# Hash bits on 32 rows, one weight tile converted behind attention, and first products ordered by feature half

## The chip, the cores and the metric

The kernel runs on one core of a Trainium2 chip. The metric is the device time of one execution in microseconds; the median of three runs is 713.83 us (713.04 to 716.22). The engines are called PE (matrix products; PEld is its weight load), DVE (vector), ACT (scalar), POOL (GpSimd) and SP (which issues most DMAs).

## The reference

Three stages follow each other. The inputs are q, k, v of shape (2, 8, 768, 64); the weights of the first mixture stage are 64-bit floats.

```python
q_bits = (np.einsum('bhsd,dk->bhsk', q, proj) > 0).astype(np.int64)      # 6 bits
k_bits = (np.einsum('bhsd,dk->bhsk', k, proj) > 0).astype(np.int64)
mask = q_bucket[:, :, :, None] == k_bucket[:, :, None, :]                # equal bits
scores = np.where(mask, scale * np.matmul(q, k.transpose(0, 1, 3, 2)), -1000000000.0)
attn = softmax(scores); attn_out = np.matmul(attn, v)
x = attn_out as (1536 tokens, 512)
x = (x @ w_a) * (x @ w_b) @ w_out                                        # 512 x 1536, 1536 x 512
out = the better of 8 experts per token: gate * relu(x @ w1[e]) @ w2[e]
```

## The kernel before

**Attention** works on eight pairs of heads. A pair's queries and keys are turned so that 128 rows hold the 64 features of both heads. `units` are (pair, head, group): 48 units of 256 queries, six to a pair. For each unit the loop of `attention` issues, for two halves of 128 queries each: scores (`scores`, L270 and L273) into one of two PSUM tiles "s", a row maximum on DVE (`rowmax`, L278), an exponential on ACT (`expo`, L284), a normalisation on POOL (`normal`, L301) and a transposition on DVE (`turn`, L308). Two units in three (u % 3 is 0 or 2) also have half of a head's product with v on PE (`pv`, L320). The third (u % 3 is 1) has a preparation for a later pair in its place: either `turned` (12 transposes, L114) or `signs` (L233, L246). The outputs of a preparation are taken by ACT in the next unit, ahead of pv. PE, DVE, ACT, POOL and SP each run their instructions in the order in which this loop writes them.

**The mask** is added to the scores as a matrix product of signs. Multiplying q and k by the projection (`lz`, its 6 columns placed in a strip for each head, zeros elsewhere) gives rows of bits; a Sign activation makes them +1 and -1 (`qf`, `sk`), and `kf` is the key signs times a large factor, one copy for each head j with zeros on the other head's rows. In a score tile (768 keys as two halves n) the scores of half n are a product on 64 rows at tile position (64n, 0), and the mask's product follows on the same 64 rows: row group n needs the query signs for all queries, so the signs of the two query halves stand in `QF` on one row group and, copied by two DMAs (L240), in `QG` on the other. For pair 0 `opening` writes them directly with ACT (L166).

**The first mixture stage** begins inside attention. `load_first` and `split64` convert weight tiles of 64-bit floats to a high and a low 32-bit part in steps that `plan` hangs on points (u, at) of the loop: fetch, rest, top (DVE), low (ACT), add (POOL), size (ACT), guard (DVE), parts (an ACT cast and a POOL subtraction). Four tiles are the first 256 columns of w_a and w_b in halves f = 0, 1 of 128 features; two more are the halves of w_out. Tiles are staged in `spare` (mid's buffers "g") or `late` (attention's buffer "raw"). `fill` says where products of the first 768 tokens (`gated_products`, L597) are issued inside and behind the loop, taken from the list `first` in order; their outputs can be `held` until a later point. Behind the loop (NU = 48) come the last pv pieces, the last epilogue, the remaining products, and then the mixture stages, where PE's order is a long list.

Of the kernel before, what the change touches and what calls it, by code (L numbers as in the profile page):

```python
# [25 lines left out]
class Kernel:  # L26
# [8 lines left out]
    def constants(self, const):  # L35
        nc = self.nc
# [8 lines left out]
        nc.vector.tensor_scalar(p[:, 1:2], p[:, 0:1], 5, 1, ALU.logical_shift_right, ALU.bitwise_and)  # L45
        nc.vector.tensor_scalar(p[:, 0:1], p[:, 0:1], 31, None, ALU.bitwise_and)
# [12 lines left out]
        self.lz = const.tile([128, 2, 2, 32], F32, name="lz")  # L59
# [4 lines left out]
    def attention(self, xh, xl, pools, hook):  # L64
# [9 lines left out]
        for tag, shape, dt, n in (  # L74
            ("et", [128, NC * S], F32, 2), ("e", [128, 2 * S], F32, 3), ("vr", [128, NC * 256], F32, 2), ("raw", [128, 2 * S], F32, 1),
            ("q", [128, S], F32, 2), ("qs", [128, S], F32, 2), ("k", [128, S], F32, 2), ("ks", [128, H2], F32, 2),
            ("xp", [128, S], F32, 2), ("co", [128, S], F32, 2), ("qf", [128, H2], BF16, 2), ("qg", [128, H2], BF16, 2), ("kf", [128, S], BF16, 2), ("sk", [128, H2], BF16, 1),
        ):
            sb.tile(shape, dt, tag=tag, name=tag, bufs=n)
        raw, Q, QS, K, KS, QF, QG, KF, VR = {}, {}, {}, {}, {}, {}, {}, {}, {}  # L80
# [56 lines left out]
        def opening():  # L137
# [6 lines left out]
            for t, tag in ((QF, "qf"), (QG, "qg")):  # L144
                t[0] = sb.tile([128, H2], BF16, tag=tag, name=tag, bufs=2)
# [39 lines left out]
            for x, r in enumerate(half):  # L185
                nc.tensor.matmul(
                    pvb[1][r, 0, :H2], lz[:, r], K[0][:, x * H2:(x + 1) * H2], start=True, stop=True, tile_position=(0, 64 * x)
                )
            sign(sk, pvb[1][:, 0, :H2])
            nc.tensor.matmul(pvb[0][:, 0, :H2], lz, Q[0][:, keys], start=True, stop=True)  # L190
            for x in range(2):
                sign((QF, QG)[x][0][half[x]], pvb[0][half[x], 0, :H2])
            for j in range(2):
                nc.vector.tensor_scalar(KF[0][:, j], sk, self.fac[:, j:j + 1], None, ALU.mult)
# [4 lines left out]
            def rest():  # L199
                nc.tensor.matmul(pvb[0][:, 1, :H2], lz, Q[0][:, queries], start=True, stop=True)  # L200

                def out(*_):
                    for x in range(2):
                        sign((QF, QG)[1 - x][0][half[x]], pvb[0][half[x], 1, :H2])
# [7 lines left out]
        def masks(eng=nc.scalar):  # L212
            for kf, sk in later:
                for j in range(2):
                    if eng is nc.scalar:
                        eng.mul(kf[:, j], sk, self.fac[:, j:j + 1])
                    else:
                        eng.tensor_scalar(kf[:, j], sk, self.fac[:, j:j + 1], None, ALU.mult)
            later.clear()

        def signs(i, n):
            p = pvb[n]
            lz = self.lz.rearrange("p a b c -> p (a b c)")
            half = [slice(64 * x, 64 * x + 64) for x in range(2)]

            def sign(dst, src):
                nc.scalar.activation(dst, src, AF.Sign, bias=self.bias[:src.shape[0]], scale=2.0 ** 100)

            if n == 0:
                QF[i] = sb.tile([128, H2], BF16, tag="qf", name="qf", bufs=2)  # L230
                QG[i] = sb.tile([128, H2], BF16, tag="qg", name="qg", bufs=2)
                for x, r in enumerate(half):
                    nc.tensor.matmul(  # L233
                        p[r, 0, :H2], lz[:, r], Q[i][:, x * H2:(x + 1) * H2], start=True, stop=True, tile_position=(0, 64 * x)
                    )

                def out(*_):
                    sign(QF[i], p[:, 0, :H2])
                    for x in range(2):
                        nc.sync.dma_start(out=QG[i][half[1 - x]], in_=QF[i][half[x]])  # L240

                return out
            KF[i] = sb.tile([128, 2, H2], BF16, tag="kf", name="kf", bufs=2)
            sk = sb.tile([128, H2], BF16, tag="sk", name="sk", bufs=1)
            for x, r in enumerate(half):
                nc.tensor.matmul(  # L246
                    p[r, 0, :H2], lz[:, r], K[i][:, x * H2:(x + 1) * H2], start=True, stop=True, tile_position=(0, 64 * x)
                )

            def out(*_):  # L250
                sign(sk, p[:, 0, :H2])
# [10 lines left out]
        def scores(u, t):  # L262
# [98 lines left out]
        for j in range(2):  # L361
            d = slice(64 * j, 64 * j + 64)
            for x in range(2):
# [13 lines left out]
        for u in range(NU + 2):  # L377
# [35 lines left out]
            if new < len(pairs):  # L413
                preps, held, held_kind = [kind(new, x) for x in ((1, 0) if kind is turned else (0, 1))], new, kind
# [46 lines left out]
class Experts:  # L461
# [16 lines left out]
    def split64(self, src, shape, dest, scratch=None):  # L478
# [45 lines left out]
        def parts():  # L524
# [3 lines left out]
            nc.gpsimd.tensor_tensor(l, v, f32(h), ALU.subtract)  # L528
# [32 lines left out]
    def load_first(self, which, f, scratch):  # L561
# [15 lines left out]
        return self.split64(src, shape, dest, scratch)  # L577
# [515 lines left out]
def tile_kernel(ctx, tc, q, k, v, proj, w_a, w_b, w_out, emb, tau, w1, w2, out, dbg=None):  # L1093
# [5 lines left out]
    with tc.manual_schedule():  # L1099
# [15 lines left out]
        with tc.tile_pool(name="conv", bufs=1, side="left") as X.conv, \  # L1115
# [10 lines left out]
            jobs = [X.load_first(w, f, spare) for f in range(2) for w in range(2)]  # L1126
            outs = [X.load_first(2, f, late) for f in range(2)]
# [224 lines left out]
```

## Time and profile before

| what | value |
|---|---|
| median of 3 runs | 713.83 us (713.04 to 716.22) |
| profiled execution | 712.7 us |
| its span, first to last instruction | 710.9 us |
| PE busy | 693.8 us (98%) |
| DVE busy | 453.6 us (64%) |
| ACT busy | 355.7 us (50%) |
| POOL busy | 435.4 us (61%) |
| mean granted PE clock | 0.998 of full speed |

The span runs from the first to the last instruction; 1.8 us of the profiled execution lie around it. Busy times of PE and PEld overlap. A row of the timeline gives a start, a duration, the engine, the line of the kernel and the operation, output and inputs, the shapes, how many instructions were merged, and in brackets how long the engine idled before it and what ended that. The profile models the end of a matmul: of one shown 0.48 us long the next may start 0.32 us behind it.

### The profile page before, as it was taken

The page shows a single profiled execution, that of the slowest core. Times are in us where ns is not written, and L with a number is a line of the kernel's source. Part 1 is how long each engine was busy: PE and PEld are TensorE (multiplying, and loading weights), DVE is VectorE, ACT ScalarE, POOL GpSimd, SP SyncE. Part 2 cuts the span into 40 slices and gives each one's busy share as a digit, 9 for nine tenths or more (in the row PEclk, how much of TensorE's full clock was granted, in tenths as well). Part 3 has the DMA queues.
Part 4 walks back from the last instruction along what each step waited for, and adds up shares of the span by engine and source line. Part 5 has one row for each costly group of instructions (what it writes and reads, how often), then busy time and mean ns, then how long its engine had stood idle before and what let it go on. Part 6 is the DMA issues. An engine that isn't in the chain of part 4 may idle for free.

```text
span 710.9 us, 16289 instructions
## 1 busy us (share of the span) xinstructions
PE 693.8 (98%) x6796; PEld 583.5 (82%) x6796; DVE 453.6 (64%) x623; ACT 355.7 (50%) x660; POOL 435.4 (61%) x439
## 2 busy tenths in 40 slices
PE   8899999999999999999999999999999999999996
PEld 5465656566689999999999999988889899989995
DVE  4899999999966636546546456335646756556640
ACT  4789888988744341211212121234546565555560
POOL 1789999989964735636726537454525766657651
PEclk9999999999999999999999999999999999999999
DMA  6947754743241311211303201633533865676500
GB/s 151 211 106 182 162 126 116 171 114 96 47 136 60 120 61 60 67 52 60 119 0 108 71 12 48 234 108 104 169 110 101 284 229 197 205 258 226 208 37 24
DMA packets 68444, 88.00 MB, mean 124 GB/s; under 512 B 28931, under 2 KB 41027, under 8 KB 68368
## 3 DMA queue, kind: packets, MB, share of 16 engines
q1 hardware_dynamic: 63728, 78.41, 37.4%
q0 software_dynamic: 2560, 7.34, 2.7%
q10 hardware_dynamic: 2080, 1.18, 0.6%
q8 instruction: 54, 0.88, 0.5%
q14 instruction: 22, 0.18, 0.1%
HBM read 75.52 MB, written 7.34 MB: 117 GB/s over the span
## 4 chain that ended last, share of the span: by engine, by line
PE 82%; DVE 6%; ACT 5%; issue 3%; DMA 2%; POOL 2%; SPq 0%; POOLq 0%; ACTq 0%; DVEq 0%
PE ab L597 26%; PE yp L629 14%; PE op L974 11%; PE hp L924 10%; PE pv L320 8%; PE st L270 5%; DVE nm L278 3%; ACT e L284 2%; DVE et L308 2%; PE part L597 1%; PE st L273 1%; PE hr L942 1%; PE xgt L901 1%; ACT xp L340 1%; ACT co L340 1%
## 5 line engine op out<-in xcount | busy, mean ns | idle before, releaser
L597 PE MATMUL ab<-xh,w 128*128 128x384 f32 x704 | 185.7, 338 | 0.0
L597 PEld LDWEIGHTS ab<-xh,w 128*128 128x128 f32 x704 | 127.7, 188 | 2.0 <-issue 1.2
L597 PE MATMUL ab<-xl,w 128*128 128x384 f32 x352 | 118.3, 336 | 0.0
L612 POOL TENSOR_TENSOR g<-a,g 128x384 fp32r<-128x384 f32 x48 | 52.5, 1094 | 102.1 <-ACT g L611 101.9
L880 POOL TENSOR_TENSOR w<-raw,w 128x1024 fp32r<-128x1024 f32 x36 | 87.9, 2446 | 38.7 <-ACT w L879 37.2
L629 PE MATMUL yp<-w,g 128*128 128x512 f32 x432 | 102.9, 390 | 0.0
L301 POOL TENSOR_SCALAR e<-e,r,mc 128x768 f32<-128x768 f32 x96 | 93.7, 983 | 10.2 <-DVE r L288 10.0
L284 ACT ACTIVATE e<-st,nm 128x768 f32<-128x768 f32 x96 | 85.7, 896 | 27.4 <-DVE r L288 14.6
L278 DVE TENSOR_REDUCE nm<-st 128x1 f32<-128x768 f32 x96 | 90.0, 943 | 11.4 <-PE st L273 11.3
L629 PEld LDWEIGHTS yp<-w,g 128*128 128x128 f32 x432 | 80.4, 188 | 14.9
L270 PE MATMUL st<-k,q 64*128 64x384 f32 x192 | 83.4, 515 | 2.2 <-ACT e L284 1.9
L308 DVE STREAM_TRANSPOSE et<-e 128x1536 f32<-128x1536 f32 x48 | 84.8, 1768 | 0.0
L270 PE MATMUL st<-ks,qs 64*128 64x384 f32 x192 | 82.8, 511 | 1.9 <-ACT e L284 1.8
L974 PE MATMUL op<-w,hth 128*128 128x512 f32 x256 | 80.7, 396 | 0.0
L924 PE MATMUL hp<-xgh,w 128*128 128x256 f32 x448 | 80.7, 281 | 0.0
L611 ACT CAST g<-a 128x384 fp32r<-128x384 f32 x48 | 24.7, 515 | 111.5 <-DVE a L610 111.5
L320 PEld LDWEIGHTS pv<-et,vr 32*64 32x64 f32 x3072 | 60.2, 130 | 17.9 <-issue 8.7
L320 PE MATMUL pv<-et,vr 32*64 32x192 f32 x3072 | 72.5, 326 | 2.0 <-ACT q L128 1.6
L880 DVE TENSOR_TENSOR w<-raw,w 128x1024 fp32r<-128x1024 f32 x28 | 64.6, 2309 | 14.6 <-ACT w L879 14.6
L924 PEld LDWEIGHTS hp<-xgh,w 128*128 128x128 f32 x448 | 69.2, 188 | 0.3
L606 ACT COPY a<-ab 128x384 f32<-128x384 f32 x44 | 21.0, 476 | 95.1 <-PE ab L597 93.8
L597 PEld LDWEIGHTS ab<-xl,w 128*128 128x128 f32 x352 | 66.2, 188 | 0.8
(218 smaller groups left out, 1243.9 us busy)
## 6 DMA issues: line engine op xcount, KB each, us to landing
raw<-in_moe_w_dram SPq DMA_DIRECT2D x32, 1024.0 KB, 5.3
vr<-in_v_dram SPq DMA_DIRECT2D x64, 192.0 KB, 3.8
raw<-in_moe_w_a_dram SPq DMA_DIRECT2D x5, 1024.0 KB, 5.1
raw<-in_moe_w_b_dram SPq DMA_DIRECT2D x5, 1024.0 KB, 4.9
raw<-in_moe_w_out_dram SPq DMA_DIRECT2D x5, 1024.0 KB, 4.8
raw<-in_k_dram SPq DMA_DIRECT2D x16, 192.0 KB, 4.0
qs<-q SPq DMA_DIRECT2D x15, 192.0 KB, 3.8
raw<-in_q_dram SPq DMA_DIRECT2D x14, 192.0 KB, 4.1
```

The lines of the kernel that those rows point to most:

```text
L270: nc.tensor.matmul(st[:, n, :H2], q[d, ql], k[d], start=True, stop=False, tile_position=(64 * n, 0))
L278: nc.vector.tensor_reduce(NM[u][:, t:t + 1], ST[u, t][:, :, :H2], axis=AX.XY, op=ALU.max, negate=True)
L284: nc.scalar.activation(halves(E[u][:, t]), ST.pop((u, t))[:, :, :H2], AF.Exp, bias=NM[u][:, t:t + 1], accum_out=SU[u][:, t:t + 1])
L301: nc.gpsimd.tensor_scalar(E[u][:, t], E[u][:, t], r[:, t:t + 1], c[:, t:t + 1], ALU.mult, ALU.add)
L308: nc.vector.transpose(ET[h][:, :, 2 * g:2 * g + 2].rearrange("p b c s -> p c b s"), E.pop(u).rearrange("p c (b s) -> p c b s", s=32),)
L320: nc.tensor.matmul(pvb[a // 2][m:m + 64, a % 2, :NC * 32], v[d], et[d, n].rearrange("p c s -> p (c s)"), start=(n < 2), stop=(n >= NB32 - ...
L597: nc.tensor.matmul(p[:, :384], w[:, k, fs], x[:, k, cols], start=(k == 0 and n == 0), stop=(k == self.KD - 1 and n == 2),)
L612: nc.gpsimd.tensor_tensor(gl[:, f], a, f32(gh[:, f]), ALU.subtract)
L629: nc.tensor.matmul(p, g[:, f, rows], w[:, f], start=(n == 0), stop=(n == 5))
L880: eng.tensor_tensor(l, raw, f32(h), ALU.subtract)
L924: nc.tensor.matmul(p[:, :256], w[:, k, fs], x[:, k], start=(n == 0), stop=(n == 3 * self.KD - 1))
L974: nc.tensor.matmul(p, h[:, 2 * n + f, rows], w[:, f], start=(n == 0 and f == 0 and m == 0), stop=(n == 3 and f == 1 and m == 2),)
```

## The change

Three things change.

1. **Hash bits.** The strip of a head in `lz` has 16 columns instead of 32, so the bits of both heads fit on 32 rows. A pair's signs come from one preparation: four products (K's two halves, Q's two halves) on the four strips of 32 columns of one PSUM bank, one Sign activation, and four DMAs that copy the two halves of Q's signs to rows 0 to 31 and to rows 32 to 63 of `QF`. `QG` is gone. The mask's products of a score tile stand on 32 rows each, at tile positions (0, 0) and (32, 0); the scores' products stay on 64 rows. `kf` is made on 64 rows.
2. **One of four weight tiles** (w_b, second feature half) is fetched near the loop's end into `late` and converted behind it, with its low part on DVE. The second half of w_out takes a buffer "e" (`weights`) and comes later still.
3. **First products** run over both token groups for feature half 0, then for half 1, so that the fourth tile is first needed behind the loop. Outputs held in units 47 and 48 are released at one point behind unit 49.

```diff
-        nc.vector.tensor_scalar(p[:, 1:2], p[:, 0:1], 5, 1, ALU.logical_shift_right, ALU.bitwise_and)
-        nc.vector.tensor_scalar(p[:, 0:1], p[:, 0:1], 31, None, ALU.bitwise_and)
+        nc.vector.tensor_scalar(p[:, 1:2], p[:, 0:1], 4, 1, ALU.logical_shift_right, ALU.bitwise_and)
+        nc.vector.tensor_scalar(p[:, 0:1], p[:, 0:1], 15, None, ALU.bitwise_and)
...
-        self.lz = const.tile([128, 2, 2, 32], F32, name="lz")
+        self.lz = const.tile([128, 4, 2, 16], F32, name="lz")
...
-            sign(sk, pvb[1][:, 0, :H2])
+            sign(sk[half[0]], pvb[1][half[0], 0, :H2])
             nc.tensor.matmul(pvb[0][:, 0, :H2], lz, Q[0][:, keys], start=True, stop=True)
-            for x in range(2):
-                sign((QF, QG)[x][0][half[x]], pvb[0][half[x], 0, :H2])
+            sign(QF[0][half[0], keys], pvb[0][half[0], 0, :H2])
...
-        def signs(i, n):
-            p = pvb[n]
+        def signs(i):
+            p = pvb[0]
...
-            for x, r in enumerate(half):
+            rows = [slice(32 * x, 32 * x + 32) for x in range(4)]
+            for x, r in enumerate(rows):
                 nc.tensor.matmul(
-                    p[r, 0, :H2], lz[:, r], K[i][:, x * H2:(x + 1) * H2], start=True, stop=True, tile_position=(0, 64 * x)
+                    p[r, 0, :H2], lz[:, r], (K, Q)[x // 2][i][:, x % 2 * H2:(x % 2 + 1) * H2],
+                    start=True, stop=True, tile_position=(0, 32 * x),
                 )
 
             def out(*_):
-                sign(sk, p[:, 0, :H2])
+                nc.scalar.activation(sk, p[:, 0, :H2], AF.Sign, bias=self.bias, scale=2.0 ** 100)
+                for y in range(2):
+                    for x in range(2):
+                        nc.sync.dma_start(out=QF[i][rows[y], x * H2:(x + 1) * H2], in_=sk[rows[2 + x]])
                 later.append((KF[i], sk))
...
-            for n, d in enumerate(rows):
-                qf = (QF if n == c // (NC // 2) else QG)[i][d, c % (NC // 2) * 128:c % (NC // 2) * 128 + 128]
-                nc.tensor.matmul(st[:, n, :H2], qf, KF[i][d, j], start=False, stop=True, tile_position=(64 * n, 0))
+            for n in range(2):
+                d = slice(32 * n, 32 * n + 32)
+                nc.tensor.matmul(st[:, n, :H2], QF[i][d, ql], KF[i][d, j], start=False, stop=True, tile_position=(32 * n, 0))
...
-            for x in range(2):
+            for x in range(4):
                 nc.vector.tensor_copy(self.lz[d, x, j, :NB], self.pr[d])
...
+        hook(NU + 3, 4)
         for col in cols:
             finish_high(end, col)
             finish_low(end, col, nc.vector)
+        hook(NU + 4, 3)
         hook(NU + 4, 0)
...
-            nc.gpsimd.tensor_tensor(l, v, f32(h), ALU.subtract)
+            (eng or nc.gpsimd).tensor_tensor(l, v, f32(h), ALU.subtract)
...
-            jobs = [X.load_first(w, f, spare) for f in range(2) for w in range(2)]
-            outs = [X.load_first(2, f, late) for f in range(2)]
+            def weights():
+                return sb.tile([128, 2 * S], F32, tag="e", name="weights", bufs=3)
+
+            jobs = [X.load_first(w, f, spare) for f, w in ((0, 0), (0, 1), (1, 0))]
+            jobs.append(X.load_first(1, 1, late, nc.vector))
+            outs = [X.load_first(2, f, (late, weights)[f]) for f in range(2)]
...
-            plan = {(-1, 0): [jobs[0][0], jobs[1][0]], (35, 1): [outs[0][0]], (45, 1): [outs[1][0]]}
+            plan = {
+                (-1, 0): [jobs[0][0], jobs[1][0]], (13, 0): [jobs[2][0]], (35, 1): [outs[0][0]], (45, 1): [jobs[3][0]],
+                (47, 4): [outs[1][0]],
+            }
             places = (
-                (3, 4, 5, 6, 6, 7, 9), (8, 8, 9, 10, 12, 13, 15), (16, 17, 18, 21, 21, 22, 27), (20, 23, 24, 28, 30, 31, 33),
-                (37, 38, 39, 40, 41, 41, 45), (NU, NU + 1, NU + 1, NU + 2, NU + 2, NU + 2, NU + 3),
+                (3, 4, 5, 6, 6, 7, 9), (8, 8, 9, 10, 12, 13, 15), (16, 17, 18, 21, 21, 22, 27),
+                (NU, NU, NU, NU, NU, NU + 1, NU + 2),
+                (37, 38, 39, 40, 41, 41, 45), (NU + 1, NU + 2, NU + 2, NU + 2, NU + 2, NU + 3, NU + 4),
             )
...
-            first = [(t, f, w, h) for t in range(2) for f in range(2) for w in range(2) for h in range(2)]
+            first = [(t, f, w, h) for f in range(2) for t in range(2) for w in range(2) for h in range(2)]
...
-                if at == 2:
+                if at == 2 and u < NU or (u, at) == (NU + 1, 4):
                     while held:
                         held.pop(0)()
```

How it moves instructions is seen in their order on an engine. First DVE behind the loop, from the transposition of the last unit but one (the second-last `et<-e` row) on; `late` before the change is the second half of w_out, after it the fourth tile; `weights` is then the second half of w_out. Before:

```order
L308 STREAM_TRANSPOSE et<-e 128x2x24x32
L610 TENSOR_TENSOR a<-part,a 128x384
L497 TENSOR_SCALAR late<-late 128x512
L308 STREAM_TRANSPOSE et<-e 128x2x24x32
L500 SCALAR_TENSOR_TENSOR late<-late 128x512
L344 TENSOR_TENSOR xp<-xp,co 64x768
L522 SCALAR_TENSOR_TENSOR late<-late 128x512
L610 TENSOR_TENSOR a<-part,a 128x384
L439 TENSOR_TENSOR xp<-pv,co 64x2x6x32 x2
```

And with the change:

```order
L291 STREAM_TRANSPOSE et<-e 128x2x24x32
L482 TENSOR_SCALAR late<-late 128x512
L485 SCALAR_TENSOR_TENSOR late<-late 128x512
L291 STREAM_TRANSPOSE et<-e 128x2x24x32
L595 TENSOR_TENSOR a<-part,a 128x384
L507 SCALAR_TENSOR_TENSOR late<-late 128x512
L482 TENSOR_SCALAR weights<-weights 128x512
L513 TENSOR_TENSOR w<-late,w 128x4x128
L327 TENSOR_TENSOR xp<-xp,co 64x768
L485 SCALAR_TENSOR_TENSOR weights<-weights 128x512
L595 TENSOR_TENSOR a<-part,a 128x384
L422 TENSOR_TENSOR xp<-pv,co 64x2x6x32 x2
```

The fourth tile's steps and its subtraction (`w<-late,w`) stand ahead of xp's addition, and the output tile's steps move behind them, the last one behind the rows shown.

Second ACT at the same place, from the last copy of a out of the loop's banks on. Before:

```order
L606 COPY a<-pv 128x384
L611 CAST g<-a 128x384
L348 CAST xh_99<-xp 128x384
L340 COPY xp<-pv 64x2x6x32
L340 COPY co<-pv 64x2x6x32
...
L606 COPY a<-part 128x384
L348 CAST xh_99<-xp 128x384
L506 ACTIVATE r_3587<-late 128x512
L516 ACTIVATE late<-late 128x512
L611 CAST g<-a 128x384
L527 CAST w<-late 128x512
```

And with the change:

```order
L591 COPY a<-pv 128x384
L491 ACTIVATE r_3562<-late 128x512
L501 ACTIVATE late<-late 128x512
L331 CAST xh_99<-xp 128x384
L323 COPY xp<-pv 64x2x6x32
L323 COPY co<-pv 64x2x6x32
...
L331 CAST xh_99<-xp 128x384
L596 CAST g<-a 128x384
L591 COPY a<-part 128x384
L512 CAST w<-late 128x4x128
L491 ACTIVATE r_3636<-weights 128x512
```

The cast of the fourth tile stands behind the epilogue's copies, one cast of xh, one of g and a copy of a.

Third SP around the copies of the query signs of pair 1 (`vr` are the loads of v, `raw` those of q and k). Before:

```order
L104 DMA qs<-q 64x768 x2
L94 DMA vr<-in_v_dram 32x4x384 x4
L240 DMA qg<-qf 64x384 x2
L87 DMA raw<-in_k_dram 128x6x64
L87 DMA raw<-in_q_dram 128x6x64
```

And with the change:

```order
L104 DMA qs<-q 64x768 x2
L94 DMA vr<-in_v_dram 32x4x384 x4
L234 DMA qf<-sk 32x384 x4
L87 DMA raw<-in_k_dram 128x6x64
L87 DMA raw<-in_q_dram 128x6x64
```

Two more issues stand at this place, ahead of the next pair's loads.

## Rows read from the trace of the kernel before

**Rows 1.** Busy time by stretch: us, then PE, PEld, DVE, ACT, POOL (instructions), clock, DMA.
```profile
34.84:195.60 160.76, 157.33 (x3314) 100.98 (x3312) 152.45 (x178) 135.12 (x281) 145.11 (x237) 1.00 0.52 125
...
219.47:710.90 491.43, 485.15 (x2863) 446.04 (x2862) 264.29 (x384) 186.83 (x315) 260.43 (x148) 1.00 0.35 120
```

**Rows 2.** Timeline, PE and PEld in a unit with pv, 132 to 137 us.
```profile
132.47 0.32 PE L273 MATMUL st<-kf,qf 64*128 64x384 bf16 x1
132.48 0.19 PEld L270 LDWEIGHTS st<-k,q 64*128 64x128 f32 x1 [0.22 <-ACT spare L516]
...
132.64 0.48 PE L270 MATMUL st<-k,q 64*128 64x384 f32 x1
...
132.96 0.48 PE L270 MATMUL st<-k,q 64*128 64x384 f32 x1
...
132.97 0.09 PEld L273 LDWEIGHTS <-qf 64*128 64x128 bf16 x1
...
133.29 0.32 PE L273 MATMUL st<-kf,qf 64*128 64x384 bf16 x1
133.54 1.86 PEld L320 LDWEIGHTS pv<-et,vr 32*64 32x64 f32 x96 [0.48 <-issue]
...
135.68 0.18 PEld L270 LDWEIGHTS st<-k,q 64*128 64x128 f32 x1 [0.28 <-issue]
...
136.10 0.48 PE L270 MATMUL st<-k,q 64*128 64x384 f32 x1
```

**Rows 3.** Timeline, DVE, the row maxima that begin units 33 and 36.
```profile
140.39 0.96 DVE L278 TENSOR_REDUCE nm<-st 128x1 f32<-128x768 f32 x1
...
151.85 0.92 DVE L278 TENSOR_REDUCE nm<-st 128x1 f32<-128x768 f32 x1
```

**Rows 4.** Timeline, ACT at the signs of one pair, and PE's next scores.
```profile
139.99 0.58 ACT L227 ACTIVATE qf<-pv,bias 128x384 bf16<-128x384 f32 x1
...
140.45 0.59 ACT L227 ACTIVATE sk<-pv,bias 128x384 bf16<-128x384 f32 x1
...
142.10 0.88 ACT L284 ACTIVATE e<-st,nm 128x768 f32<-128x768 f32 x1
...
143.29 0.59 PE L270 MATMUL st<-ks,qs 64*128 64x384 f32 x1
```

**Rows 5.** Timeline, opening, second sign passes on ACT and the mask product.
```profile
11.47 0.58 ACT L166 ACTIVATE qg<-pv,bias 64x384 bf16<-64x384 f32 x1
...
12.10 0.33 PE L273 MATMUL st<-kf,qg 64*128 64x384 bf16 x1 [0.27 <-ACT qg L166]
...
15.82 0.58 ACT L166 ACTIVATE qf<-pv,bias 64x384 bf16<-64x384 f32 x1
```

**Rows 6.** Timeline, SP's copies of the query signs of pair 1 and their use.
```profile
29.73 1.11 SPq L240 DMA_DIRECT2D qg<-qf  x2
...
34.47 0.33 PE L273 MATMUL st<-kf,qg 64*128 64x384 bf16 x1 [0.97 <-DMA qg<-qf]
```

**Rows 7.** Timeline, unit 23: a step of the fourth tile on DVE, then pv.
```profile
105.16 0.68 DVE L500 SCALAR_TENSOR_TENSOR spare<-spare 128x512 int32<-128x512 int32 x1
...
106.05 2.21 PE L320 MATMUL pv<-et,vr 32*64 32x192 f32 x96 [0.32 <-ACT q L128]
```

**Rows 8.** Timeline behind the loop, 206 to 217 us: DVE, ACT and a product.
```profile
206.56 1.20 DVE L500 SCALAR_TENSOR_TENSOR late<-late 128x512 int32<-128x512 int32 x1
...
208.13 0.47 ACT L340 COPY co<-pv 64x384 f32<-64x384 f32 x1
...
210.95 0.45 PE L597 MATMUL part<-xh,w 128*128 128x384 f32 x1
...
211.78 0.69 DVE L522 SCALAR_TENSOR_TENSOR late<-late 128x512 f32<-128x512 f32 x1 [2.19 <-POOL late L511]
...
214.35 0.61 ACT L527 CAST w<-late 128x512 fp32r<-128x512 f32 x1
...
216.02 1.02 DVE L439 TENSOR_TENSOR xp<-pv,co 64x384 f32<-64x384 f32 x2 [2.12 <-ACT co L438]
```

More of the change, by code (lines that the diff above doesn't have):

```diff
@@ L143, in opening @@
                 t[0] = sb.tile([128, n], F32, tag=tag, name=tag, bufs=2)
-            for t, tag in ((QF, "qf"), (QG, "qg")):
-                t[0] = sb.tile([128, H2], BF16, tag=tag, name=tag, bufs=2)
+            QF[0] = sb.tile([128, S], BF16, tag="qf", name="qf", bufs=2)
             KF[0] = sb.tile([128, 2, H2], BF16, tag="kf", name="kf", bufs=2)
@@ L202, in out @@
                 def out(*_):
-                    for x in range(2):
-                        sign((QF, QG)[1 - x][0][half[x]], pvb[0][half[x], 1, :H2])
+                    sign(QF[0][half[0], queries], pvb[0][half[0], 1, :H2])
                 return out
@@ L223, in signs @@
             lz = self.lz.rearrange("p a b c -> p (a b c)")
[L224 to L242, printed above, removed]
+            QF[i] = sb.tile([128, S], BF16, tag="qf", name="qf", bufs=2)
@@ L248, in signs @@
                 )
             def out(*_):
-                sign(sk, p[:, 0, :H2])
+                nc.scalar.activation(sk, p[:, 0, :H2], AF.Sign, bias=self.bias, scale=2.0 ** 100)
+                for y in range(2):
+                    for x in range(2):
+                        nc.sync.dma_start(out=QF[i][rows[y], x * H2:(x + 1) * H2], in_=sk[rows[2 + x]])
                 later.append((KF[i], sk))
@@ L362, in attention @@
             d = slice(64 * j, 64 * j + 64)
-            for x in range(2):
+            for x in range(4):
                 nc.vector.tensor_copy(self.lz[d, x, j, :NB], self.pr[d])
@@ L413, in attention @@
             if new < len(pairs):
-                preps, held, held_kind = [kind(new, x) for x in ((1, 0) if kind is turned else (0, 1))], new, kind
+                preps, held, held_kind = [turned(new, x) for x in (1, 0)] if kind is turned else [signs(new)], new, kind
             elif s != 1 and u >= 5:
@@ L475, in __init__, with split64 @@
         self.yT, self.sel, self.mx, self.rps, self.HS, self.RW = ({} for _ in range(6))
-    def split64(self, src, shape, dest, scratch=None):
+    def split64(self, src, shape, dest, scratch=None, eng=None):
         nc = self.nc
@@ L559, in load_gated, with load_first @@
         return jobs
-    def load_first(self, which, f, scratch):
+    def load_first(self, which, f, scratch, eng=None):
         K = self.K
@@ L575, in dest @@
             return [t[:, :, 128 * f:128 * f + 128] if which < 2 else t[:, f:f + 1] for t in self.WG[0, which]]
-        return self.split64(src, shape, dest, scratch)
+        return self.split64(src, shape, dest, scratch, eng)
     def gated_products(self, c, t, f, which, half, psum=None, held=None):
@@ L1136, in tile_kernel @@
                 for m, u in enumerate(us):
-                    plan.setdefault((u, 3 if m in (3, 4, 6) else 4), []).append(steps[m])
-            plan[13, 0], plan[16, 0] = [jobs[2][0]], [jobs[3][0]]
-            first = [(t, f, w, h) for t in range(2) for f in range(2) for w in range(2) for h in range(2)]
+                    at = 1 if u == NU else 4 if u == NU + 2 and m < 6 else 3 if m in (3, 4, 6) else 4
+                    plan.setdefault((u, at), []).append(steps[m])
+            first = [(t, f, w, h) for f in range(2) for t in range(2) for w in range(2) for h in range(2)]
             fill = {40: 2, 43: 2, 46: 2, 47: 2, NU: 2, NU + 3: 2, NU + 4: 4}
```

16 lines of the change are left out of this document (7 added, 9 removed).

## The prediction, made before the changed kernel was run

> **What bounds the kernel now.** I read the trace by stretches first [rows 1]. Behind attention (from 219 us on) PE is busy for 485 of 491 us and the change leaves that part alone, so whatever it is worth shows before 220 us. From the seventh unit's row maximum (34.84) to the last one's (195.60) PE is busy 157.3 and DVE 152.5 of 160.8 us: two engines near their limit, with POOL (145) and ACT (135) behind them.
>
> Next, the timeline of a unit with a pv piece [rows 2]. The scores products and the mask products stream one behind the other, pv's loads start at 133.54, the next scores loads at 135.68, and PE waits for no other engine. PE is the bound of such a unit, and two units in three are of this kind. The third kind (turns or signs instead of pv) is short on PE. The row maxima show the sum [rows 3]: 140.39 to 151.85, 11.46 us for three units without a conversion step on DVE, the last of them reached with no wait on DVE. The whole stretch, 41 units, is 4.1 us above 41/3 x 11.46 = 156.6; that is what conversion steps on DVE and some late hand-overs cost.
>
> Rows 2 also show how PE passes from one tile shape to another. Between 64x128 tiles the next weight load starts 0.01 us behind the mask product's start (132.48 against 132.47), and the next scores product 0.17 behind it: no gap. At the passage to the 32x64 tiles of pv the load waits: the mask product of 133.29 has streamed by about 133.45, the load starts at 133.54, so 0.09 are lost. Coming back, the first pass of the scores takes 0.42 (135.68 to 136.10) where one in the stream takes 0.32 (132.64 to 132.96): 0.10 more, since its load isn't hidden.
>
> **The change, part by part.**
>
> *Mask products on 32 rows.* The scores products keep 64-row tiles; each pair of mask products behind them now takes two 32-row tiles. I expect the passages of rows 2 there: 0.09 in, 0.09 for emptying on the way out (taken equal to the way in), 0.10 for the exposed load, together 0.28 us. The trace holds no passage from 64x128 to 32x128, so I bound it. Zero, or a shade of gain, if it costs nothing while all columns stay; 0.37, if the mask's own load (0.09, at 132.97) is exposed as well. I take 0.28, for the pv passages are the nearest rows. In a pv unit the first pair pays the whole round trip; the second pays only the way in, which pv behind it then doesn't pay again: zero. Two pv units in three of 41: 27 x 0.28 = 7.6 us. Part of that hides under the 4.1 us by which other work stretches the loop today; I take half, 2.0. In the third kind of unit, and in the pv piece behind a turn, PE has room: pv waits there for ACT's copy of q (106.05) [rows 7]. **+5.6 us**, bounds 0 and 27 x 0.37 = 10.0.
>
> The Trainium skill, "TensorEngine Tiling (Array Packing)", Key Properties, says that changing the tiling mode, and not just the tile, drains TensorE, and its list has 64-row and 32-row tiling as different modes. That speaks against this change. It gives no price; rows 2 agree with it for the passages they hold.
>
> *Signs.* One ACT pass replaces two for each of seven pairs. The second starts 0.46 behind the first (139.99, 140.45) [rows 4], so 7 x 0.46 = 3.2 us leave ACT. The exponential behind them (142.10) frees the scores' room while PE is still in pv, until 143.29. I count **0**, with -3.2 as the good end. The sign products now stand on four column strips at once; PE saves time there that it would spend waiting for ACT's exponential. Factor products on 64 instead of 128 rows keep their columns: 0. Four more tiny copies of the projection go ahead of DVE's first large work, which waits for PE: 0.
>
> *Opening.* The second mask product waits for the second sign pass (11.47, 0.58 long; product at 12.10) [rows 5]. With one pass it starts 0.58 earlier, and the first row maximum with it. The other half's second pass (15.82) goes too, another 0.2. **-0.8 us**, bounds -1.2 and 0.
>
> *Copies of the query signs.* SP issues four DMAs of 32 rows where two of 64 took 1.11 us [rows 6], so about 2.2. For pair 1 someone waits: the mask product at 34.47 had stood 0.97 for the first copy, issued from 29.73. It now needs the first and the third, issued 1.1 later. The first landed 4.7 us after its issue, so it stood behind other loads, and the third may land close behind it. **+0.6**, bounds 0 and 1.1. Later pairs are prepared several units ahead. What follows in SP's queue starts 1.1 us later; there it is loads for later units.
>
> *The fourth tile's conversion leaves the loop.* DVE loses three steps like the one at 105.16 [rows 7], at most 3 x 0.68 = 2.0 us, ACT and POOL three and two. In units that PE bounds this buys nothing: behind that very step PE started pv at 106.05 because of ACT. **-0.3**, bounds -2.0 and 0.
>
> *Behind the loop.* PE has the same products in another order. New is that the fourth tile must be ready for the product that starts at 210.95 [rows 8]. On ACT the epilogue's last copy starts at 208.13 and ends by 208.6; behind it stand two casts, a copy of a and the tile's own cast, each between 0.47 and 0.61: 210.5 to 211.0. DVE's subtraction, new there, is bounded by two steps of its size, 0.69 (211.78) and 1.20 (206.56): 211.2 to 212.2. The third matmul needs it, two passes of 0.17 behind 210.95, at 211.3. **+0.2**, bounds 0 and 0.9. DVE waits for that cast with two pieces queued behind it: the output tile's second step and xp's addition, whose other half comes only at 216.02. The output tile's last step on DVE now stands behind those additions (216.02, 1.02 long), so its cast, today at 214.35, comes about 218, and its subtraction on POOL ends about 220, just when the output product's second half wants it. I count 0 for that.
>
> Sum: 5.6 - 0.8 + 0.6 - 0.3 + 0.2 = +5.3 us. The profiled execution took 712.7 us, which gives 718.0. The median of the runs shown is 713.83, 1.1 above that execution; on it I forecast **719.2 us**.
>
> **Rivals.**
> 1. *The passage costs nothing.* For it: the mask tiles lie inside rows that the scores tiles use, and all columns stay. Against it: every change of shape in rows 2 has its gap. Then -0.8 + 0.6 - 0.3 + 0.2 = -0.3: **713.5 us**, no change. The Trainium skill, "TensorE: Matmul & The Clock Gate", Part 3, lets PE pull a weight load ahead of running matmuls when it goes to the background weights; carried over to this passage it is this rival, and rows 2 contradict it wherever the shape changes.
> 2. *ACT was the bound*, so the shorter sign passes come off the path: not slower but faster. Place: the unit behind the signs. Price: 3.2 for the signs and 2.0 for the conversion steps, with the opening's 0.8 and 0.8 to pay elsewhere: 713.8 - 5.2 = **708.6 us**. It decides only if PE stands ready when ACT does the signs; rows 4 show PE in pv until 143.29, after the exponential's start.
> 3. *PE stops behind the loop.* If the fourth tile's fetch or DVE's wait comes 1.5 us later than worked out, PE stands at 210.95 and again before the output product, together some 2.3 us: with rival 1, **715.8 us**.
>
> **How the numbers follow.** Passages paid 0.63; rival 1 0.25; rival 2 0.07; rival 3 0.05. The likeliest case's own range is 716 to 723. The range for all, 712.5 to 722.5, leaves out rival 2, the low edge of rival 1 and the full 0.37 with nothing hidden, about 0.19. A measurement of this kernel can tell about 0.5% (3.6 us) from no change. Slower by more means over 717.4: four fifths of the first case and a little of rival 3, 0.52. Faster by more, under 710.2, is rival 2 and an edge, 0.08. The rest, 0.40, is no change.
>
> **What would show it.** In the changed profile the mask loads would start about 0.1 us behind the end of the scores products and the next scores loads about 0.1 behind the masks; three units without conversion would take about 12.0 us, and DVE's waits for scores would grow. If mask loads start inside the scores products and three units stay near 11.4, the passage term is wrong and rival 1 holds. If the product that now starts at 210.95 waits over 1 us for w, rival 3 is in it. Three units well under 11 would speak for rival 2.

## The result, and the profile after

The changed kernel takes **725.3 us** (median of 4 runs, 724.02 to 725.59), against 715.0 of the kernel before in the same sitting (713.04 to 716.22): ratio **1.0143**, interval 1.0113 to 1.0174. Slower, as forecast, but by nearly twice the forecast: some 10.2 us instead of 5.4. 725.3 lies above the range's end of 722.5. The profiled execution has a span of 722.2 us, 11.3 over the 710.9 of before.

First the stretches of the changed kernel, cut as in [rows 1]: from the seventh unit's row maximum to the last one's, and the part behind attention (us, then PE, PEld, DVE, ACT, POOL busy with their instructions, granted clock, DMA share, GB/s).

```profile
35.09:206.67 171.58, 168.62 (x3314) 96.20 (x3316) 154.65 (x176) 134.07 (x273) 142.78 (x237) 1.00 0.48 114
230.46:722.20 491.74, 485.12 (x2861) 445.64 (x2860) 260.94 (x384) 187.36 (x315) 262.14 (x149) 1.00 0.36 119
```

The 41 units take 171.58 instead of 160.76 us, **+10.8**. TensorE has 11.3 us more of busy time in them; DVE has 2.2 more, ACT and POOL a little less than before. Up to the seventh unit 0.25 are lost (35.09 against 34.84), and from the last row maximum to the end 0.2 (515.5 against 515.3). 0.25 + 10.8 + 0.2 is the whole difference of the spans. The granted clock is 1.00 in both kernels' stretches.

Next the same kind of unit as in [rows 2], PE and PEld.

```profile
133.35 0.48 PE L253 MATMUL st<-k,q 64*128 64x384 f32 x1
...
133.77 0.09 PEld L256 LDWEIGHTS <-qf 32*128 32x128 bf16 x2 [0.55 <-issue]
133.77 0.34 PE L256 MATMUL st<-kf,qf 32*128 32x384 bf16 x2
134.03 0.18 PEld L253 LDWEIGHTS st<-k,q 64*128 64x128 f32 x1 [0.17 <-issue]
134.04 0.59 PE L253 MATMUL st<-k,q 64*128 64x384 f32 x1
...
134.46 0.48 PE L253 MATMUL st<-k,q 64*128 64x384 f32 x1
...
134.88 0.09 PEld L256 LDWEIGHTS <-qf 32*128 32x128 bf16 x2 [0.55 <-issue]
...
135.15 1.86 PEld L303 LDWEIGHTS pv<-et,vr 32*64 32x64 f32 x96 [0.17 <-ACT q L128]
...
137.28 0.18 PEld L253 LDWEIGHTS st<-k,q 64*128 64x128 f32 x1 [0.28 <-ACT e L267]
...
137.71 0.48 PE L253 MATMUL st<-k,q 64*128 64x384 f32 x1
```

Each change of tile shape is now a step in these rows.
- Scores to mask: the last scores pass starts at 133.35, streams 0.32, and the mask's load comes at 133.77. 0.10 are lost.
- Mask to scores: the mask products, side by side, start at 133.77; the next load comes 0.26 later. In [rows 2] the next product started 0.17 behind a mask product, so 0.09 are lost, and the first scores pass (134.04 to 134.46) again takes 0.42 instead of 0.32, because its load is exposed: 0.10 more.
- Scores to mask in the second pair: 134.46 + 0.32 = 134.78, the load at 134.88. Again 0.10.
- Mask to pv: 135.15 is 0.26 behind the start of the mask product. In [rows 2] the passage from the 64-row mask to pv took 0.25. So 32x128 to 32x64 is a passage too, no cheaper than the old one. The row names ACT's copy of q as what ended the wait, but that copy had ended at 134.96, and the same 0.26 stands in all 28 pv units of the stretch, most of which wait for nothing that the profile shows.

Together about 0.4 us a unit. The row maxima on DVE show it as a sum: here are those that begin units 19 to 22, with no conversion step among them, and the mask products and the second row maximum of unit 20.

```profile
88.98 0.96 DVE L261 TENSOR_REDUCE nm<-st 128x1 f32<-128x768 f32 x1 [0.24 <-PE st L256]
...
92.97 0.33 PE L256 MATMUL st<-kf,qf 32*128 32x384 bf16 x2
...
93.35 0.96 DVE L261 TENSOR_REDUCE nm<-st 128x1 f32<-128x768 f32 x1 [0.61 <-PE st L256]
...
94.08 0.33 PE L256 MATMUL st<-kf,qf 32*128 32x384 bf16 x2
...
94.46 0.96 DVE L261 TENSOR_REDUCE nm<-st 128x1 f32<-128x768 f32 x1
...
97.03 0.92 DVE L261 TENSOR_REDUCE nm<-st 128x1 f32<-128x768 f32 x1
...
101.30 0.96 DVE L261 TENSOR_REDUCE nm<-st 128x1 f32<-128x768 f32 x1 [0.61 <-PE st L256]
```

The kernel before has these rows at the same places, between the two of [rows 3] (units 34 and 35):

```profile
144.41 0.96 DVE L278 TENSOR_REDUCE nm<-st 128x1 f32<-128x768 f32 x1 [0.45 <-PE st L273]
...
148.00 0.32 PE L273 MATMUL st<-kf,qf 64*128 64x384 bf16 x1
...
148.36 0.96 DVE L278 TENSOR_REDUCE nm<-st 128x1 f32<-128x768 f32 x1 [0.38 <-PE st L273]
...
148.81 0.32 PE L273 MATMUL st<-kf,qf 64*128 64x384 bf16 x1
...
149.31 0.94 DVE L278 TENSOR_REDUCE nm<-st 128x1 f32<-128x768 f32 x1
```

Three units take 12.32 us, where [rows 3] had 11.46 and the prediction named about 12.0 for its likeliest case. A pv unit takes 4.37 (88.98 to 93.35), where one bound by PE took 3.95 (144.41 to 148.36). The third kind takes 3.68 (93.35 to 97.03), where it took 3.49 (148.36 to the 151.85 of [rows 3]). At the row maxima that begin units 20 and 22 DVE stands 0.61 us for the scores; at the like rows of the kernel before (148.36, 144.41) it stood 0.38 and 0.45.

The third kind lengthens on another path than the pv units. DVE runs such a unit's two row maxima and a transposition one behind the other, before the change with no idle time shown up to the next unit. The second pair's mask products came 0.81 behind the first pair's (148.00, 148.81), in time for the second row maximum, 0.95 behind the first (148.36, 149.31). Now they come 1.11 behind (92.97, 94.08), and so does the second row maximum (93.35, 94.46).

Three more places that the prediction named: the opening ([rows 5]), the copies of pair 1's query signs ([rows 6]), and the fourth tile behind the loop ([rows 8]).

```profile
11.78 0.09 PEld L256 LDWEIGHTS <-qf 32*128 32x128 bf16 x2 [0.55 <-ACT qf L165]
...
12.16 0.96 DVE L261 TENSOR_REDUCE nm<-st 128x1 f32<-128x768 f32 x1 [0.21 <-PE st L256]
...
29.79 2.48 SPq L234 DMA_DIRECT2D qf<-sk  x4
...
34.30 0.76 PE L256 MATMUL st<-kf,qf 32*128 32x384 bf16 x2 [0.82 <-DMA qf<-sk]
...
212.85 0.68 ACT L491 ACTIVATE r<-late 128x512 int32<-128x512 uint32 x1 [2.31 <-DMA late<-in_moe_w_b_dram]
...
221.14 0.69 DVE L513 TENSOR_TENSOR w<-late,w 128x512 fp32r<-128x512 f32 x1 [2.50 <-ACT w L512]
...
252.55 3.25 PE L614 MATMUL yp<-w,g 128*128 128x512 f32 x13 [0.31 <-POOL g L597]
```

The first mask products come 0.32 earlier than in [rows 5]. The first mask product of pair 1 waits about as long for the copied signs as before (0.82, 0.97). Behind the loop ACT waits 2.31 for the fetched tile and DVE 2.50 for ACT's cast; PE waits for neither, and only at 252.55 stands 0.31 for POOL's g, the low part of the gated products.

### The profile page after: what moved, and what is told of

It is laid out like the page before. It is cut to its first block, busy times and chain, and to the rows that moved or that the text cites. A ratio compares the mean times of both kernels' runs of the same rounds, so it can differ in the third digit from the quotient of the medians.

```text
span 722.2 us, 16280 instructions
## 1 busy us (share of the span) xinstructions
PE 706.0 (98%) x6796; PEld 577.7 (80%) x6796; DVE 456.2 (63%) x628; ACT 355.5 (49%) x651; POOL 435.2 (60%) x438
## 4 chain that ended last, share of the span: by engine, by line
PE 87%; ACT 4%; issue 3%; DVE 3%; DMA 2%; POOL 1%; SPq 0%; POOLq 0%; ACTq 0%; DVEq 0%
PE ab L582 24%; PE yp L614 13%; PE op L959 11%; PE hp L909 10%; PE pv L303 9%; PE st L253 9%; PE st L256 3%; ACT e L267 1%; PE part L582 1%; PE pv L582 1%; PE pv L114 1%; PE hr L927 1%; PE xgt L886 1%; DMA raw<-in_k_dram 1%; ACT co L323 1%
## 5 line engine op out<-in xcount | busy, mean ns | idle before, releaser
L597 POOL TENSOR_TENSOR g<-a,g 128x384 fp32r<-128x384 f32 x48 | 56.8, 1184 | 96.4 <-ACT g L596 96.4
L261 DVE TENSOR_REDUCE nm<-st 128x1 f32<-128x768 f32 x96 | 91.6, 954 | 21.1 <-PE st L256 17.6
L253 PE MATMUL st<-ks,qs 64*128 64x384 f32 x192 | 87.2, 534 | 4.9 <-ACT e L267 4.9
L253 PE MATMUL st<-k,q 64*128 64x384 f32 x192 | 87.3, 535 | 1.4 <-ACT e L267 1.2
L619 DVE TENSOR_TENSOR y<-yp,y 128x512 f32<-128x512 f32 x60 | 41.5, 692 | 39.5 <-PE yp L614 39.4
```

The costliest lines, as they stand in the source:

```text
L253: nc.tensor.matmul(st[:, n, :H2], q[d, ql], k[d], start=True, stop=False, tile_position=(64 * n, 0))
L261: nc.vector.tensor_reduce(NM[u][:, t:t + 1], ST[u, t][:, :, :H2], axis=AX.XY, op=ALU.max, negate=True)
L597: nc.gpsimd.tensor_tensor(gl[:, f], a, f32(gh[:, f]), ALU.subtract)
```

## The experiments

Theory A: every change of the tile shape on TensorE (PE) costs about 0.1 us (0.2 into the scores), and that is the whole loss. Rival B: the sign part, its copies or the moved conversion cost it. Rival C: the 32-row products are dear by themselves, not the change of shape. Ratios are to the kernel before, run beside each group; its medians were 713.8 to 715.0 us, so ratios are compared rather than times. "Loop" is the stretch from the seventh unit's first row maximum to the last one's in the profiled execution, one for each kernel. In e4, e7 and e10 it holds a fall of the granted clock, told at the end.

| run | us | ratio, 95% interval | loop |
|---|---|---|---|
| before | 713.8 to 715.0 | 1 | 160.8 |
| changed | 725.3 | 1.0143 [1.0113, 1.0174] | 171.6 |
| e1 32-row masks alone | 724.4 | 1.0166 [1.0143, 1.0189] | 171.8 |
| e2 hash bits alone | 724.4 | 1.0155 [1.0134, 1.0177] | 171.8 |
| e3 conversion and order alone | 712.1 | 0.9988 [0.9969, 1.0006] | 160.5 |
| e4 changed, 64-row masks | 712.5 | 0.9987 [0.9968, 1.0007] | 163.1 |
| e5 32 rows, first pair only | 720.0 | 1.0091 [1.0077, 1.0105] | 167.9 |
| e6 32 rows, second pair only | 715.5 | 1.0024 [1.0014, 1.0034] | 162.5 |
| e7 changed, mask first in second pair | 720.5 | 1.0085 [1.0072, 1.0098] | 169.6 |
| e8 e4 with v loaded later | 711.8 | 0.9973 [0.9961, 0.9984] | 161.1 |
| e9 32 rows, third kind of unit only | 715.9 | 1.0028 [1.0014, 1.0041] | 163.6 |
| e10 32 rows, pv units only | 721.3 | 1.0101 [1.0082, 1.0121] | 169.8 |
| e11 before with v loaded later | 714.1 | 0.9997 [0.9986, 1.0008] | 161.8 |
| e12 e3 with v loaded later | 713.4 | 0.9987 [0.9977, 0.9998] | 163.6 |

### Which part of the change (e1 to e4)

e1 is the smallest edit that holds the suspected passage: in the kernel before, a head's bits already fill just 32 of the 64 rows.

```diff
-            for n, d in enumerate(rows):
+            for n in range(2):
+                d = slice(64 * n + 32 * j, 64 * n + 32 * j + 32)
...
-                nc.tensor.matmul(st[:, n, :H2], qf, KF[i][d, j], start=False, stop=True, tile_position=(64 * n, 0))
+                nc.tensor.matmul(st[:, n, :H2], qf, KF[i][d, j], start=False, stop=True, tile_position=(64 * n + 32 * j, 0))
```

> The kernel before with one edit: each mask product contracts only the 32 rows of its own head (the other 32 rows are zero there anyway) on a 32x128 tile. Hash layout, sign passes, DMAs and the weight tiles' conversion are the old ones. Theory A (changes of TensorE's tile shape are the whole loss): a pv unit goes from 3.95 to about 4.36 us, the third kind from 3.49 to about 3.7, the loop is 10 to 11 us longer, 714.5 + 10.5 = 725 us. Rival B (the passage costs little, the loss comes from the new sign part, its DMAs or the conversion): under 717 us.

e2 takes the change's attention part, e3 its other part (weight conversion, order of the first products), each on the kernel before.

> The changed kernel's hash bits alone: 16 bits a head, one sign product round and one sign pass for keys and queries, four copies, mask products on 32 rows; conversion and order of the first products as before. Theory A: all of the loss is here, 724 to 726 us. Rival B (a good part of the loss comes from the conversion behind the loop): 718 to 721 us, the rest in the complement.

> The changed kernel without its hash bits: the fourth weight tile converted behind the loop and the first products ordered by feature half, on the old attention. Theory A: 714.5 - 0.5 = 714 us, between 713 and 715.5 (0.3 gained in the loop, up to 0.6 lost behind it). Rival B: 718 us or more, with TensorE standing near 210 or near 240 us.

e4 keeps the whole change but gives the mask products their 64 rows back (in the opening the sign products too); rows without bits are zero. Its central lines:

```diff
-                    p[r, 0, :H2], lz[:, r], (K, Q)[x // 2][i][:, x % 2 * H2:(x % 2 + 1) * H2],
+                    p[r, 0, :H2], lz[:, r], (K, Q)[x % 2][i][:, x // 2 * H2:(x // 2 + 1) * H2],
...
-                        nc.sync.dma_start(out=QF[i][rows[y], x * H2:(x + 1) * H2], in_=sk[rows[2 + x]])
+                        nc.sync.dma_start(out=QF[i][rows[2 * y], x * H2:(x + 1) * H2], in_=sk[rows[1 + 2 * x]])
...
-                d = slice(32 * n, 32 * n + 32)
-                nc.tensor.matmul(st[:, n, :H2], QF[i][d, ql], KF[i][d, j], start=False, stop=True, tile_position=(32 * n, 0))
+                d = rows[n]
+                nc.tensor.matmul(st[:, n, :H2], QF[i][d, ql], KF[i][d, j], start=False, stop=True, tile_position=(64 * n, 0))
```

> The changed kernel with its one sign pass, four copies and moved conversion, but with the mask products back on 64-row tiles: the keys' bits stand at rows 0 and 64, the queries' bits at rows 32 and 96 of the sign tile, and the factors are zero on the other rows. Theory A: no change of shape between scores and mask products, so a pv unit is back at 3.95 us and the time at 714 us or a little under (the third kind of unit has fewer sign products), 711 to 714.5. Rival B (signs, DMAs or conversion cost the time): stays above 720 us.

e1, with nothing of the new sign part, its copies or the conversion in it, loses as much as the whole change; its loop is 171.8 us like that of the changed kernel. e4, with all of these but without the passage, loses nothing. So B falls from both sides. The rest of the change is worth nothing that can be measured, alone (e3) or with the masks on 64 rows (e4): both intervals include 1. e3's 712.1 us lies under theory A's 713 to 715.5, but so near before that it can't be told from it. PE and PEld of a unit in e4:

```profile
91.27 0.10 PEld L261 LDWEIGHTS <-qf 64*128 64x128 bf16 x2
...
91.59 0.33 PE L261 MATMUL st<-kf,qf 64*128 64x384 bf16 x2
91.59 0.19 PEld L258 LDWEIGHTS st<-k,q 64*128 64x128 f32 x1 [0.22 <-issue]
...
91.75 0.48 PE L258 MATMUL st<-k,q 64*128 64x384 f32 x1
92.07 0.48 PE L258 MATMUL st<-k,q 64*128 64x384 f32 x1
```

The mask's load is back under the scores pass (91.27), the scores' load starts with the mask product (91.59), and the first scores pass is 0.32 again (91.75 to 92.07).

### Change of shape or 32-row product (e5 to e7)

e5 and e6 are e1 with `if t == 0 else rows[n]` and `if t == 1 else rows[n]` behind the slice (t is the pair). e7 is the changed kernel with the second pair's order turned round; of a score tile's two steps, whichever comes first now begins the accumulation:

```diff
...
+            for step in (products, mask) if t == 0 else (mask, products):
+                step()
```

> The kernel before, with 32-row mask products in the first pair of each unit alone; the second pair's stay on 64 rows. Two more changes of shape a unit (scores to mask, mask to scores). Theory A, prices read from the changed kernel's trace (0.09 in, 0.10 for emptying, 0.10 for the exposed load = 0.29): 27 pv units x 0.29 = 7.9, the third kind of unit 14 x 0.1 = 1.4, some 2.5 hidden: +6.8, about 720.5 us. The step on record (only the first pair pays): +10 to 11 us, 724.5. Rival C (each pair of 32-row products costs by itself, not the change of shape): half of the loss, +5.3, 719.

> The kernel before, with 32-row mask products in the second pair of each unit alone. One more change of shape a unit (scores to mask; mask to pv stands where scores to pv stood). Theory A: 27 x 0.11 = 3.0, third kind 14 x 0.1 = 1.4, 1.5 to 2 hidden: +2.5, about 716.3 us. The step on record (the second pair pays nothing): 713.8 us. Rival C: +5.3, 719 us.

> The changed kernel with the second pair's mask products put ahead of its scores products, so that they stand right behind the first pair's masks, on the same tile shape. As many 32-row products as in the changed kernel, one change of shape a unit fewer. Theory A: like the first pair alone, a pv unit at about 4.25 us, 720.5 to 722 us. Rival C (each pair of 32-row products costs by itself): no change, 724.4 us.

e5 and e6 have equally many 32-row products and differ in the changes of shape, two more than before against one: +0.91% and +0.24%. By the row maxima the commonest length of a pv unit is 4.26 in e5 and 4.06 in e6, where one bound by PE took 3.95: +0.31 and +0.11; with both (e1), 4.36. e7 has as many 32-row products as the changed kernel and one change of shape less, and it is at 4.26 and 720.5 us. So C falls. PE and PEld of one pv unit in e5, e6 and e7, in turn:

```profile
94.58 0.09 PEld L274 LDWEIGHTS <-qf 32*128 32x128 bf16 x1 [0.55 <-issue]
...
94.84 0.18 PEld L270 LDWEIGHTS st<-ks,qs 64*128 64x128 f32 x1 [0.17 <-issue]
...
95.85 1.86 PEld L321 LDWEIGHTS pv<-et,vr 32*64 32x64 f32 x96 [0.48 <-ACT sk L227]
...
97.99 0.18 PEld L270 LDWEIGHTS st<-ks,qs 64*128 64x128 f32 x1 [0.28 <-issue]
```

```profile
94.87 0.48 PE L270 MATMUL st<-ks,qs 64*128 64x384 f32 x1
...
95.29 0.09 PEld L274 LDWEIGHTS <-qf 32*128 32x128 bf16 x1 [0.55 <-issue]
...
95.56 1.86 PEld L321 LDWEIGHTS pv<-et,vr 32*64 32x64 f32 x96 [0.17 <-ACT sk L227]
```

```profile
90.11 0.50 PE L259 MATMUL st<-kf,qf 32*128 32x384 bf16 x4
90.54 0.18 PEld L254 LDWEIGHTS st<-k,q 64*128 64x128 f32 x1 [0.32 <-issue]
...
91.39 2.21 PE L309 MATMUL pv<-et,vr 32*64 32x192 f32 x96
...
93.52 0.59 PE L254 MATMUL st<-k,q 64*128 64x384 f32 x1
```

In e5 the load of the scores waits until 0.26 behind the mask's, as in the changed kernel, and pv follows a 64-row mask. In e6 the mask's load waits for the scores (the last pass starts at 94.87 and streams 0.32; the load comes 0.10 behind that), and pv's load comes 0.27 behind it. In e7 both pairs' masks run as one group (x4, at 90.11), with the scores 0.43 behind its start and one emptying for both. e6's 715.5 us is 1.6 above before, between the 0 of the step on record and A's 716.3, and its interval excludes 0 and C's 719. e5's 720.0 agrees with A's 720.5 and is 1 above C's number; the three runs together leave only A.

### Which units pay (e9, e10)

e1 again, with `if u % 3 == 2 else rows[n]` (scores ahead of turns or signs) and with `if u % 3 != 2 else rows[n]` (ahead of pv).

> The kernel before, with 32-row mask products in both pairs, but only in the scores that stand ahead of turns or signs (the third kind of unit, a third of all). Theory A (a unit of this kind is also bound by TensorE in part: 3.49 became 3.68): 14 x 0.19 = 2.7, of which the loop's slack hides about half: +1 to +1.5 us, 715 us; a unit of this kind then lasts 3.6 to 3.7. The step on record (TensorE has room in these units): 0, 713.9 us.

> The kernel before, with 32-row mask products in both pairs, but only in the scores that stand ahead of a pv piece (two thirds of all). Theory A: 27 x 0.41 = 11.2, less up to 3 hidden: +8 to +9.5 us, 722 to 723 us. The step on record with its price of 0.28 a unit, 2.0 of it hidden: +5.6, 719.5 us.

The third kind pays as well: +0.28%, 2.0 us, and its units lengthen to 3.68. The pv units alone give +1.0%, 7.2 us, a little under A's number: 27 x 0.41 = 11.1 less 7.2 is 3.9, nearly all of the 4.1 by which other work stretches the loop. e9 and e10 together (9.2) fall short of e1 (11.9), as e5 and e6 do (8.2). That each part alone hides under the same 4.1 fits these numbers, but no run tests it.

### A version that beats both (e8, e11, e12)

In e4's profile the seventh unit's mask product waited 2.07 us for the query signs' copies, and the clock fell behind it (the rows stand at the end). e8, e11 and e12 issue the second head's load of v a unit later, on e4, on the kernel before, and on e3:

```diff
-            if s == 0 and u >= 3 and u // 3 < 2 * len(pairs):
+            if s == 0 and u > 3 and u // 3 < 2 * len(pairs) or u == 4:
```

> The changed kernel with the mask products on 64 rows, and the second head's load of v issued one unit later, behind the copies of the second pair's query signs. With the mask products on 64 rows alone, the mask product of the seventh unit waited 2.1 us for these copies, which stood behind that load. If the load in front is what holds them, the wait falls under 1 us and the time to 710.5 to 711.5 us, under the kernel before; if the copies take their time by themselves, it stays at 712.5 us.

> The kernel before with nothing changed but the second head's load of v, issued one unit later, behind the copies of the second pair's query signs. If the gain of the version with 64-row masks and the later load is that of the wait alone (1.0 us in the profiled execution of before, up to 2.1 in others, then also a lower granted clock): 711.8 to 712.8 us, the wait at the seventh unit's mask product gone. If it needs the new sign part: 713.9, no change.

> The same later load of v on the kernel with the old sign part and the moved conversion with its order of the first products. If the two savings add up: 710.5 to 711.5 us, the fastest version here. If the moved conversion is worth nothing in the time, the same as the later load alone, 712 to 712.8 us.

e8 has the lowest ratio here: 711.8 us, 0.9973, interval 0.9961 to 0.9984, 1.7% below the changed kernel. The gain over before is less than the 0.5% of the prediction, but the interval excludes 1. The wait is gone, as expected; the time is 0.3 above the 710.5 to 711.5 that was expected with it. In its profile the seventh unit's row maximum comes at 33.27 (34.84 before), the loop takes 161.1 (160.8), and from the last row maximum to the end it takes 514.9 (515.3). The later load alone is a miss: in e11 the wait at the mask product is gone, and the time is the same. Rows of PE in e11, the seventh unit's mask product without a wait and the second pv piece behind it:

```profile
33.56 0.32 PE L273 MATMUL st<-kf,qf 64*128 64x384 bf16 x1
...
39.05 1.85 PE L320 MATMUL pv<-et,vr 32*64 32x192 f32 x72
41.81 0.88 PE L320 MATMUL pv<-et,vr 32*64 32x192 f32 x24 [0.90 <-issue]
```

A new wait has come for the old one: the last quarter (x24 of 96) of the pv piece that starts at 39.05 stands 0.90 us. The trace names nothing that it waits for. The later load isn't it: this piece is the second half of the first head's product, and the load that moved is the second head's. e12 has a stop of 0.95 at the same piece, e8 has none; what it is stays open. e12 (713.4 us, 0.9987) is no better than e3 and misses both numbers expected of it. So what e8 has over before is not the later load alone; how it divides over sign part, order and load is left open, since the intervals of e3, e4 and e8 overlap.

## Why the prediction was wrong in size

The mechanism and the sign were right, and the likeliest case was the right one. The step that failed is the first term, *mask products on 32 rows*, put at +5.6 us with bounds 0 and 10.0. The loop measured +10.8 with the whole change and +11.0 with the 32-row masks alone (e1). Two parts of that term were put at nothing and are not nothing: the second pair of a pv unit, and the third kind of unit. Each is about 2.7 us before anything hides, together about the 5.2 that were missing.

- *The price of a round trip, 0.28 us from pv's passages.* Right: 0.31 in e5, and the rows of the changed kernel show its three parts of about 0.1. Reading a price for 64x128 to 32x128 from the rows of 64x128 to 32x64 was sound. Rival 1 (the passage costs nothing) fell; mask loads start 0.10 behind the scores, as the prediction said they would if the term held. The Trainium skill's "TensorEngine Tiling (Array Packing)", Key Properties (changing the tiling mode drains TensorE), agrees with these rows, which add the price.
- *"The second pair pays only the way in, which pv behind it then doesn't pay again: zero."* Wrong. It took 32x128 and 32x64 as one shape because the rows are the same. They are two: pv's load waits for the mask product as it did for the 64-row one. The second pair pays 0.10 a unit (0.10 in the rows, 4.06 against 3.95 in e6), 27 x 0.10 = 2.7 us before any of it hides.
- *"In the third kind of unit, and in the pv piece behind a turn, PE has room."* Right for the pv piece and wrong for the unit. Five pv pieces behind a turn, like that of [rows 7], waited 0.32 us for ACT's q before; none does now, so part of the added work hides there. The unit of the turn or of the signs lengthened from 3.49 to 3.68, 14 x 0.19 = 2.7 us, and its masks cost 2.0 us alone (e9). PE's room doesn't help it, for the path runs through DVE: the second row maximum has to wait for the second pair's masks. [Rows 7], on which that step stood, are a pv piece behind a turn and not the unit of the turn.
- *Half of it hides, 2.0.* Near: 27 x 0.41 + 14 x 0.19 = 13.7 us of added work make 10.8, so about 3 hid. (27 and 14 are the prediction's count; the row maxima show 28 pv units and 13 others, which adds 0.2.) The half was a guess from no row, so that it came near is luck.
- *The upper bound, 27 x 0.37.* It rested on the same two steps as the value, so it moved with them and was no bound. With the two counted and nothing hidden it is 13.7, the sum 13.4, and that end 727 us.

The other terms. (All terms together make 719.1, not the 719.2 written down.) *Opening, -0.8:* the first mask product came 0.32 and the first row maximum 0.31 earlier, and by the seventh unit it was gone. The row itself said so: in [rows 5] the product stood 0.27 for the second sign pass, and the term took the pass's length (0.58) in place of the wait. *Copies, +0.6:* the first row maximum of the seventh unit is 0.25 later, opening's gain included. That isn't the copies alone, since the units ahead of it pay changes of shape too, and the wait itself differs far more from profile to profile than the term is large: none (e1) to 1.60 us (e6) with the old copies, 0.54 (e2) to 2.07 (e4) with the new. *Fourth tile, -0.3, and behind the loop, +0.2:* e3 has the two together at 0.9988, no change that can be told, as forecast. From the last row maximum on, the profiles of e3, e4, e7, e8 and e12, which all have the moved conversion, take 514.8 to 515.0 us, the changed kernel's 515.5, before's 515.3; so the changed kernel's +0.2 there is no price of the moved conversion. ACT waits 2.31 for the tile, DVE 2.50 for ACT's cast, and PE needs neither then, so rival 3 (PE stops behind the loop) fell. The 0.31 at 252.55, in the output product's second half, is a wait for POOL's g and not for the tile; e10, without the moved conversion, stands 0.30 for POOL's g at 252.34 of its profile, and those five don't. *Rival 2 (ACT was the bound)* fell: e4 has the short sign passes and gains nothing that can be measured.

## What to carry to other kernels

In these rows the tile shape on TensorE is rows and columns: count every change of either in a unit of the loop, here at about 0.1 us each, and another 0.1 where the first load of the scores is exposed behind it. Small products that save rows were dear between large ones of another shape. Padding them with zero rows to the neighbours' shape took the whole loss away (e4); grouping them took part of it (e7, +0.85% instead of +1.43%). Room on one engine does not help where another engine waits for its work, as DVE does in the third kind of unit. And work out the bound of a term with its zeros taken out: a bound that keeps the same "pays nothing here" as the value is the value again.

## What was not expected of the hardware

A wait was paid for a second time, by the clock. In e4's profile PE had little to do at 32 to 36 us, because it waited for the copied signs (busy 0.77 and 1.16 of 2 us each), and then the granted clock fell. In stretches of 2 us (the third number from the right is the granted clock):

```profile
32.00:34.00 2.00, 0.77 (x4) 0.15 (x3) 1.26 (x1) 2.00 (x5) 1.41 (x4) 1.00 1.05 199
34.00:36.00 2.00, 1.16 (x6) 0.62 (x8) 0.49 (x1) 0.56 (x2) 0.00 (x0) 0.92 0.73 165
36.00:38.00 2.00, 2.00 (x37) 1.14 (x40) 1.76 (x4) 1.23 (x3) 1.35 (x2) 0.50 1.13 254
38.00:40.00 2.00, 2.00 (x74) 1.56 (x58) 1.42 (x1) 1.33 (x3) 1.76 (x5) 0.73 1.07 261
```

```profile
34.84 0.63 PE L261 MATMUL st<-kf,qf 64*128 64x384 bf16 x2 [2.07 <-DMA qf<-sk]
...
36.67 3.36 PE L308 MATMUL pv<-et,vr 32*64 32x192 f32 x96
```

A clock of 0.50 is the 1.2 GHz level. The pv piece took 3.36 us instead of 2.21, and the unit 5.57 instead of about 4. Of e4's twelve executions the three with a mean granted clock of 0.995 or 0.996 took 715.4 to 716.6 us, the nine others 710.8 to 713.4. The profiles of e7 and e10 show the same (PE busy 0.56 and 0.47 us at 34 to 36, then a granted clock of 0.51 and 0.50 at 38 to 40); e6, busy 0.53 at 34 to 36, kept 1.00. e10 has the old copies, so this is no matter of the change: the wait in the seventh unit comes with both layouts, and where it is long it can be paid twice.
